# Value products in four 32-row tiles, probabilities without zero blocks, the memory rows turned in two halves, and a new order of the work

## The chip, the cores and the metric

The kernel runs on one core of a Trainium2 chip. The metric is device time in microseconds (us), from start to end of one execution. Engines are called as the profile calls them: PE (matmul) with PEld (its weight loads), DVE (vector), ACT (scalar), POOL (GpSimd) and SP, which issues most DMAs.

## The reference

Sequence 2048, model width 512, 32 heads of 128, memory of 8 rows, segments of 32 rows. The attention is recurrent over 64 segments: each segment attends over its own rows and 8 memory rows, and the first 8 output rows are the memory of the next one.

```python
for s in range(n_seg):                       # 64 segments, one after the other
    xs = x[:, s * seg_len:(s + 1) * seg_len, :]
    h = jnp.concatenate([mem, xs], axis=1)   # 8 + 32 rows
    q, k, v = [jnp.einsum('btd,dhe->bhte', h, W) for W in (Wq, Wk, Wv)]
    scores = jnp.einsum('bhqe,bhke->bhqk', q, k) * scale
    scores = jnp.where(mask[None, None], scores, -1000000000.0)   # memory rows see the memory; all else is causal
    p = _softmax(scores, axis=-1)
    o = jnp.einsum('bhqk,bhke->bhqe', p, v)
    o = jnp.einsum('bhte,hed->btd', o, Wo)
    mem = o[:, :M, :]
    outs.append(o[:, M:, :])
...
h  = x + _A_ref(_layernorm(x), ...)
h2 = h + _B_ref(_layernorm(h), ...)          # layernorm again, w1 (512 x 1792), gelu, w2
```

The mask line of the reference is `(idx[:, None] < M) | (idx[:, None] >= idx[None, :])`: memory rows see every key of their segment, the others see the keys up to their own.

## The kernel before

**Phases.** From 0 to about 44 us the weights arrive. From about 44 to 717 us the 64 segments run, one every 10.3 us. The rest is the second half of the network (w1, gelu, w2) over all rows.

**A segment.** A segment's work on PE is a list of named parts, all in program order on PE:

- `Q0`, `K0`, `Q1`, `K1`, `V0`, `V1`: the projections, by halves of 16 heads. Each is four passes, one for each 128-row chunk of the width; a pass is four matmuls of 512 columns in four 32-column tiles of the array (L872; L605 where the weights of the pass before are kept). `hT` holds the segment's 32 rows turned: 24 rows of x that come early, and 8 memory rows that come from the segment before.
- `SC0`, `SC1` (L1037): the scores of the 8 memory rows, 16 heads each. Their softmax is `sc_softmax`: maximum, two exponentials on ACT with their sums (L1054), reciprocals (L1059), normalized probabilities `PC` (L1062), and a 32x32-blockwise transpose on DVE into `PTC` (L1064).
- `PV0`, `PV1` (`pv_c`, L1075 and L1080): probabilities times values for the memory rows. `VS` holds the values with the keys of four groups of heads on the partitions, 32 each. The products are made in two 64-row tiles of the array; `PC` therefore holds two groups side by side with the other group's block at zero (`even`), and each product has 32 columns (16 wanted and 16 that pair with the zero block), or 128 for the eight rows that come from the next segments' block (`VBD`). The results lie in banks 0 and 1 of the PSUM tile `quad`. One copy brings the memory rows to `OT` (`OTm`), one brings rows of the last part of each segment to `OTB`.
- `SA` (L1105): scores of the 24 x rows, whose softmax ends in `PA` on POOL (L1126), a transpose to `PTA` on DVE (L1128), and four POOL copies (L1132) that lay out `BD`, block-diagonal with zeros. `PVA` (`pv_a`, L1143) multiplies it with the values of the segment before, in 64-row tiles, 48 columns each, into banks 2 and 3; two copies (`OTx0`, `OTx1`) bring it to `OT`. It runs one segment late; the x rows of `OT` are used in `WO` another segment later.
- `WO` (L1171): the output projection, eight units of eight matmuls of 256 columns. Units 0 to 3 need `OTm0`, units 4 to 7 `OTm1`. Its result lies in bank 7. DVE transposes all 256 columns (L1183) and adds the two halves into the memory rows of the next segment's `hT` (L1177, two instructions); this releases the next `Q0`.
- `F0`, `F1`: passes for a whole block of rows (four segments), which no segment waits for at once. They fill PE's time where a chain on the other engines is under way.

**What sets the order.** `ORDERS` has one list for each of four segments in turn (called orders 0 to 3 here), by which PE's parts are cut and laid in a row: `('F1', 2, 3)` is pass 2 of `F1`. The other engines' operations are put in order by a planner (`schedule`): it takes operations by the key of `PLAN`, puts each in the first gap of its engine by modelled durations, and where an operation may run on several engines takes the earliest end, unless `HOME` names one. `op` derives every wait from the tiles and PSUM banks read and written; a bank counts as one thing, and a reader of a bank holds it against later readers too. SC0 and SC1 lie in banks 3 and 2. Banks of the rest: `BANK` (L42), where `K0`, `V0` and `WO` share bank 7.

**Instruction blocks.** PE's instructions are counted (`align`) in blocks of 256; `PHASE` says at which place in a block a segment is to begin, and extra weight loads (L870) pad towards it.

## Time and profile before

| What | Value |
|---|---|
| Time, median of 3 runs | 807.96 us (807.1 to 808.1) |
| Profiled execution: span from first to last instruction | 805.9 us |
| Profiled execution's own time | not listed beside its span; the runs lie 1.2 to 2.2 us above that span |
| PE busy | 775.0 us, 96% of the span |
| DVE busy | 621.0 us, 77% |
| ACT busy | 527.1 us, 65% |
| POOL busy | 349.6 us, 43% |
| Mean granted PE clock | 0.993 |

A busy PE is not a PE at its peak: matmuls overlap in the pipeline, and a matmul that takes 380 ns from start to end occupies its place in the stream for a much shorter time. So pieces of PE's work are measured here from the start of one to the start of the next. A line of a timeline gives the start and the length of a merged piece, engine, source line, operation, the tile written and the tiles read, and how many instructions were merged.

### The profile page before, as it was taken

To read this page: it belongs to the slowest core of one execution; us is meant where nothing else is said; L and a number is where in the kernel's file an instruction comes from. 1 tells how busy PE (TensorE), PEld (TensorE's weight loads), DVE (VectorE), ACT (ScalarE), POOL (GpSimd) and SP (SyncE) were. 2 spreads that over 40 slices of the span, in tenths; PEclk is the share of its full clock that TensorE was granted. 3 is DMA by queue.
4 is the path that set the end of the run, shared out by engine and by line. 5 is a ranking of instruction groups with operands and counts; after the bars stand their busy time and mean duration, and the time that the engine had idled before them with its cause. 6 is when DMAs were issued, how large, how long until landed. Compare 5 with 4: busy or idle time off the path is not lost.

```text
span 805.9 us, 43594 instructions
## 1 busy us (share of the span) xinstructions
PE 775.0 (96%) x19308; PEld 422.5 (52%) x18891; DVE 621.0 (77%) x2008; ACT 527.1 (65%) x1522; POOL 349.6 (43%) x886
## 2 busy tenths in 40 slices
PE   3788999999999999999999999999999999999998
PEld 1345555555555555555555555555555555544443
DVE  3268897989898989898989898989899887824211
ACT  2446777777777777777777777777676766643342
POOL 5023334545454545454545454545463535267200
PEclk9989999999999999999999999999999999999999
DMA  9950010111101010101010202020212131264200
GB/s 340 392 185 16 4 29 11 30 31 29 31 21 39 17 43 17 43 11 50 9 45 10 50 11 50 11 49 3 51 29 62 40 86 29 88 170 130 69 27 26
DMA packets 65449, 48.03 MB, mean 60 GB/s; under 512 B 29028, under 2 KB 61676, under 8 KB 65260
## 3 DMA queue, kind: packets, MB, share of 16 engines
q1 hardware_dynamic: 64928, 44.98, 19.0%
q8 instruction: 150, 2.46, 1.2%
q14 instruction: 39, 0.32, 0.1%
q10 hardware_dynamic: 332, 0.27, 0.1%
HBM read 31.08 MB, written 8.13 MB: 49 GB/s over the span
## 4 chain that ended last, share of the span: by engine, by line
PE 91%; DVE 3%; DMA 2%; SPq 2%; ACT 1%; issue 1%; POOL 0%
PE ps L872 43%; PE ps L1171 16%; PE ps L605 6%; PE quad L1579 6%; PE ps L1572 5%; PE ps L1210 4%; PE quad L1075 3%; DMA WQ<-in_A_Wq_dram 2%; SPq L775 2%; PE ps L1105 2%; PE quad L1037 2%; PE ps L1365 2%; PE quad L1143 1%; PE quad L1080 1%; DVE PC L1062 1%; ACT kq L890 1%
## 5 line engine op out<-in xcount | busy, mean ns | idle before, releaser
L872 PE MATMUL ps<-WQ,hT 128*32 128x512 bf16 x2048 | 157.4, 382 | 3.4 <-DVE hT L1177 3.3
L1171 PE MATMUL ps<-WO,OT 128*32 128x256 bf16 x4224 | 140.8, 275 | 1.0 <-ACT OT L890 1.0
L872 PE MATMUL ps<-WV,hT 128*32 128x512 bf16 x1780 | 138.7, 379 | 0.0
L891 ACT ACTIVATE kq<-ps 128x512 bf16<-128x512 f32 x146 | 87.2, 597 | 63.7 <-PE ps L872 63.4
L1126 POOL TENSOR_TENSOR PA<-SA,rsa 128x256 bf16<-128x256 f32 x64 | 39.9, 624 | 183.0 <-DVE rsa L1119 170.6
L890 ACT CAST kq<-ps 128x512 bf16<-128x512 f32 x160 | 93.4, 584 | 38.2 <-PE ps L872 38.2
L1171 PEld LDWEIGHTS ps<-WO,OT 128*32 128x32 bf16 x4224 | 96.2, 97 | 26.5 <-ACT OT L890 12.3
L1132 POOL COPY BD<-PTA 32x192 bf16<-32x192 bf16 x256 | 95.5, 373 | 16.6 <-DVE PTA L1128 0.8
L1062 DVE SCALAR_TENSOR_TENSOR PC<-EC,rsc,even 128x128 bf16<-128x128 f32 x256 | 94.5, 370 | 6.7
L872 PE MATMUL ps<-WK,hT 128*32 128x512 bf16 x1292 | 92.5, 379 | 0.0
L872 PEld LDWEIGHTS ps<-WQ,hT 128*32 128x32 bf16 x2048 | 57.0, 96 | 57.9 <-issue 18.7
L913 DVE STREAM_TRANSPOSE KALL<-kq 128x256 f32<-128x256 f32 x160 | 70.5, 440 | 20.8 <-ACT kq L890 18.6
L1054 ACT ACTIVATE EC<-quad,nmc 128x64 f32<-128x64 f32 x252 | 77.1, 311 | 5.9 <-DVE nmc L1045 0.2
L605 PE MATMUL ps<-WK,hT 128*32 128x512 bf16 x756 | 74.6, 379 | 0.0
L890 ACT CAST VS<-ps 128x512 bf16<-128x512 f32 x126 | 73.7, 585 | 0.7
L890 ACT CAST OT<-quad 128x128 bf16<-128x128 f32 (+1 forms) x205 | 66.3, 363 | 7.5 <-PE quad L1080 5.7
L913 DVE STREAM_TRANSPOSE QT<-kq 128x256 f32<-128x256 f32 x128 | 57.0, 445 | 15.5 <-ACT kq L891 14.1
L872 PEld LDWEIGHTS ps<-WV,hT 128*32 128x32 bf16 x1780 | 50.5, 96 | 34.2 <-issue 1.0
L1575 ACT ACTIVATE WQ<-ps,b1t 128x512 bf16<-128x512 f32 x42 | 28.9, 688 | 52.0 <-PE ps L1572 52.0
L872 PEld LDWEIGHTS ps<-WK,hT 128*32 128x32 bf16 x1292 | 36.4, 97 | 46.1 <-issue 20.1
L1117 ACT ACTIVATE SA<-SA 128x256 f32<-128x256 f32 x64 | 26.7, 417 | 49.4 <-DVE SA L1116 45.0
L1223 POOL TENSOR_TENSOR opT<-TTB,TTS 32x64 bf16<-32x64 f32 x128 | 40.3, 315 | 31.7 <-DVE opT L1177 22.5
(160 smaller groups left out, 1477.9 us busy)
## 6 DMA issues: line engine op xcount, KB each, us to landing
WV<-in_A_Wv_dram SPq DMA_DIRECT2D x4, 1024.0 KB, 10.3
WK<-in_A_Wk_dram SPq DMA_DIRECT2D x4, 1024.0 KB, 18.0
WQ<-in_A_Wq_dram SPq DMA_DIRECT2D x4, 1024.0 KB, 19.0
WO<-in_A_Wo_dram SPq DMA_DIRECT2D x16, 256.0 KB, 7.6
v_last<-VSB SPq DMA_DIRECT2D x60, 64.0 KB, 3.1
VBD<-v_last SPq DMA_DIRECT2D x60, 64.0 KB, 2.8
h_mid<-xr SPq DMA_DIRECT2D x16, 128.0 KB, 1.8
WQ<-h_mid SPq DMA_DIRECT2D x4, 512.0 KB, 4.4
```

What stands on the lines that cost most here:

```text
L605: return e.add_instruction(mybir.InstMatmult(name="I-%d" % (4000000 + _kept[0]), engine=mybir.EngineType.PE, start_tensor_calc=start, stop ...
L872: ins = e.matmul(o, l, m, start=(k == 0), stop=(k == DC - 1), tile_position=(0, 32 * j), skip_group_check=True)
L890: return {"act": (lambda e: e.copy(out, src), t_act(n, ps_)), "dve": (lambda e: e.tensor_copy(out, src), 0.155 + 1.0e-3 * n * fast)}
L891: return {"act": (lambda e: e.mul(out, src, scale_), t_act(n, ps_)), "dve": (lambda e: e.tensor_scalar(out, src, scale_, None, ALU.mult), ...
L913: S.op("dve", lambda e: e.transpose(out, src), reads=[("kq", i)], writes=[key], dur=t_dve(256) + 0.02)
L1054: return e.activation(EC[:, r, sl, :], o[:, sl, :], ACTF.Exp, bias=nmc[:, r, sl:sl + 1], accum_out=smc[:, r, sl:sl + 1])
L1062: S.op("dve", lambda e, sl=sl, xc=xc: e.scalar_tensor_tensor(PC[:, r, :, :, sl], xc, rsc[:, r, sl:sl + 1], ev, ALU.mult, ALU.mult), reads= ...
L1132: S.narrow(S.op("pool", lambda e, j=j, rows=rows: e.tensor_copy(BD[rows, par, :, j, :, :], PTA[rows, :, 0:NA, :]), reads=["PTA"], writes=[ ...
L1171: ins = e.matmul(ps[bank][32 * j:32 * j + 32, 0:256], lhs(slot(h)), wo_cols(h, b), start=(k == 0), stop=(k == 15), tile_position=(0, 32 * ...
L1223: return e.tensor_tensor(o[32 * q:32 * q + 32, c:c + 2], x, y, ALU.add)
L1572: ins = e.matmul(ps[bank][:, 0:SBT], W1[:, cc, fc * P:(fc + 1) * P], hnT_of(k)[:, cc, :], start=(cc == 0), stop=(cc == DC - 1))
L1579: S.op("pe", lambda e: e.matmul(quad[:, t, :], gT_of(k, fc)[:, t * P:(t + 1) * P], W2[:, fc, :], start=(fc == 0), stop=(fc == FC - 1)), re ...
```

## The change

1. `pv_c` and `pv_a` work in four 32-row tiles, each with a bank of `quad` of its own: 16 products of 16 columns and 4 of 64 for each `PV` (before: 8 of 32 and 2 of 128), 32 of 24 for `PVA` (before: 16 of 48). `PC` and `PTC` are half as wide and have no zero blocks; `BD`, its four POOL copies and `even` are gone, and `PVA` reads `PTA`.
2. `PV0`, `PV1` and `PVA` now write all four banks. `PVA` runs ahead of `PV0`; its two copies run after `PV1`, between `OTm1` and `OTB`.
3. `WO`'s result is turned and added in two halves of two chunks (`TT2`): `hTl`, then `hTm`; each pass waits for its chunk's half alone.
4. In `k_seg` the second half of the keys is copied and turned in two pieces (`KSPLIT`).
5. `ORDERS`, `PLAN`, `HOME`, `PHASE` and `SLIP` are new. `WO` is in one piece behind `PV1`; in orders 0 and 3 three F passes instead of four stand behind `WO`; the prefills of SA are named for DVE in orders 0, 2 and 3.

```diff
-FETCH_AT, PADS, SLIP = 65, 8, 24
-PHASE = (0, 64, 128, 192)
+FETCH_AT, PADS, SLIP = 65, 8, 80
+PHASE = (0, 128, 0, 128)
+TT2, KSPLIT, PCTS, NORM2, OTMS = True, True, False, True, False
...
-ORDERS = ((('Q0', 0, 1), ('K0', 0, 1), ('Q0', 1, 2), ('K0', 1, 2), ('Q0', 2, 3), ('Q1', 0, 1), ('Q0', 3, 4), ('K0', 2, 4), ('Q1', 1, 4), ('K1', 0, 4), ('SC0', 0, 99), ('V0', 0, 1), ('V1', 0, 1), ('V0', 1, 4), ('F1', 0, 1), ('SC1', 0, 99), ('V1', 1, 2), ('F1', 1, 2), ('V1', 2, 4), ('F0', 0, 1), ('PV0', 0, 99), ('PVA', 0, 99), ('F1', 2, 3), ('WO', 0, 2), ('PV1', 0, 99), ('WO', 2, 8), ('F1', 3, 4), ('SA', 0, 99), ('F0', 1, 4)),
...
+ORDERS = ((('Q0', 0, 2), ('K0', 0, 3), ('Q0', 2, 4), ('K0', 3, 4), ('Q1', 0, 4), ('K1', 0, 4), ('SC0', 0, 99), ('V1', 0, 1), ('V0', 0, 4), ('F1', 0, 1), ('SC1', 0, 99), ('F1', 1, 2), ('V1', 1, 4), ('F1', 2, 3), ('F0', 0, 1), ('PVA', 0, 99), ('PV0', 0, 99), ('F1', 3, 4), ('PV1', 0, 99), ('WO', 0, 8), ('F0', 1, 4), ('SA', 0, 99)),
+          (('Q0', 0, 1), ('K0', 0, 2), ('Q0', 1, 4), ('K0', 2, 4), ('Q1', 0, 4), ('K1', 0, 4), ('SC0', 0, 99), ('V1', 0, 1), ('V0', 0, 4), ('F1', 0, 1), ('SC1', 0, 99), ('F1', 1, 3), ('V1', 1, 4), ('PVA', 0, 99), ('PV0', 0, 99), ('F1', 3, 4), ('PV1', 0, 99), ('WO', 0, 8), ('SA', 0, 99), ('F0', 0, 4)),
+          (('Q0', 0, 1), ('K0', 0, 2), ('Q0', 1, 4), ('Q1', 0, 1), ('K0', 2, 4), ('Q1', 1, 4), ('K1', 0, 4), ('SC0', 0, 99), ('V1', 0, 1), ('V0', 0, 4), ('F1', 0, 1), ('SC1', 0, 99), ('V1', 1, 3), ('F1', 1, 3), ('V1', 3, 4), ('PVA', 0, 99), ('PV0', 0, 99), ('F1', 3, 4), ('PV1', 0, 99), ('WO', 0, 8), ('SA', 0, 99), ('F0', 0, 4)),
+          (('Q0', 0, 1), ('K0', 0, 2), ('Q0', 1, 4), ('K0', 2, 4), ('Q1', 0, 4), ('K1', 0, 4), ('SC0', 0, 99), ('F0', 0, 1), ('V0', 0, 4), ('V1', 0, 1), ('SC1', 0, 99), ('V1', 1, 4), ('F0', 1, 4), ('PVA', 0, 99), ('PV0', 0, 99), ('F1', 0, 1), ('PV1', 0, 99), ('WO', 0, 8), ('F1', 1, 2), ('SA', 0, 99), ('F1', 2, 4)))
...
-PLAN = {"kq2": (1.72,) * 4,
...
+PLAN = {"EC0": (-0.197, 2.191, -0.625, -6.415),
...
-HOME = {('SC0', 0): 'act', 'ZCm0': 'pool', 'kq1': 'act', 'SP1': 'act', 'VS1': 'act', 'OTm0': 'act', 'SAp': 'dve', 'PA': 'pool', 'VSB1': 'act'}
+HOME = {'SP1': 'act', 'SAp': 'dve', ('SA', 2): 'dve', 'ZCm1': 'pool', 'OTx0': 'act', 'PA': 'pool', ('SC1', 0): 'act', 'ZCm0': 'pool', ('SA', 0): 'dve', ('SC0', 2): 'act', ('SC1', 3): 'dve', 'kq2': 'act', 'kq0': 'act', ('SA', 3): 'dve', 'VSB1': 'dve', 'OTm1': 'act', 'VSB0': 'act', 'VS0': 'act', 'OTm0': 'act', ('SC0', 0): 'dve'}
...
-        PC = sb("PC", [P, 2, 2, 64, 2])
-        PTC = sb("PTC", [P, 2, 2, 64, 2])
+        PC = sb("PC", [P, 2, 64, 2])
+        PTC = sb("PTC", [P, 2, 64, 2])
-        BD = sb("BD", [P, 2, 4, 4, NA, 2])
...
+        HT = ("hTl", "hTl", "hTm", "hTm") if TT2 else ("hTm",) * 4
+        HK = ("hTl", "hTm") if TT2 else ("hTm",)
...
+            if r == 1 and KSPLIT and s > 0:
+                for h, (a, b) in enumerate((("kql", "KAl"), ("kq", "KA"))):
+                    c = slice(4 * h, 4 * h + 4)
+                    S.either(copy2(kq[:, r, c], ps[bank][:, 256 * h:256 * h + 256].rearrange("p (a b e) -> p a e b", a=4, b=2), 256), reads=[("ps", bank)], writes=[(a, r)])
+                    src = kq[:, r, c].rearrange("p a e b -> p a (e b)").bitcast(F32)
+                    S.op("dve", lambda e, h=h, src=src: e.transpose(words(KALL[:, a0 + 4 * h:a0 + 4 * h + 4]), src), reads=[(a, r)], writes=[(b, par, r)], dur=0.31)
+                return
...
-            for sl, names in enumerate((("Ea", "sa", "ra", "PCa"), ("EC", "smc", "rsc", "PC"))):
-                ek, sk, rk, pk = [(n, r) for n in names]
-                S.op("dve", lambda e, sl=sl: e.reciprocal(rsc[:, r, sl:sl + 1], smc[:, r, sl:sl + 1]), reads=[sk], writes=[rk], dur=0.16)
-                x = EC[:, r, sl, :]
-                xc = bass.AP(x.tensor, x.offset, [list(x.ap[0]), [0, 2], [1, 64]])
-                S.op("dve", lambda e, sl=sl, xc=xc: e.scalar_tensor_tensor(PC[:, r, :, :, sl], xc, rsc[:, r, sl:sl + 1], ev, ALU.mult, ALU.mult),
-                     reads=[ek, rk, "even"], writes=[pk], dur=0.305)
-            S.op("dve", lambda e: e.transpose(PTC[:, r].rearrange("p k t a -> p (k t a)").bitcast(F32), PC[:, r].rearrange("p k t a -> p (k t a)").bitcast(F32)),
-                 reads=[("PCa", r), ("PC", r)], writes=[("PTC", r)], dur=0.31)
+            if NORM2:
+                for sl, names in enumerate((("Ea", "sa", "ra", "PCa"), ("EC", "smc", "rsc", "PC"))):
+                    ek, sk, rk, pk = [(n, r) for n in names]
+                    S.op("dve", lambda e, sl=sl: e.reciprocal(rsc[:, r, sl:sl + 1], smc[:, r, sl:sl + 1]), reads=[sk], writes=[rk], dur=0.16)
+                    f = lambda e, sl=sl: e.tensor_scalar(PC[:, r, :, sl], EC[:, r, sl, :], rsc[:, r, sl:sl + 1], None, ALU.mult)
...
+            S.op("dve", lambda e: e.transpose(PTC[:, r].rearrange("p t a -> p (t a)").bitcast(F32), PC[:, r].rearrange("p t a -> p (t a)").bitcast(F32)),
+                 reads=[("PC", r)] + [("PCa", r)] * NORM2, writes=[("PTC", r)], dur=0.25)
...
-                    for t in range(2):
-                        rows = slice(64 * t, 64 * t + 64)
+                    for j in range(4):
+                        rows = slice(32 * j, 32 * j + 32)
                         c0 = 16 * (i % 2)
-                        o = quad[:, t, 128 * r:128 * r + 128].rearrange("p (b i q) -> p i b q", b=2, i=4)[:, i]
-                        e.matmul(o, VS[rows, s % 3, r, i * E:(i + 1) * E], PTC[rows, r, :, c0:c0 + 16, i // 2],
-                                 start=(r == 0 and i == 0), stop=False, tile_position=(64 * t, 0), skip_group_check=True)
-                for t in range(2):
-                    rows = slice(64 * t, 64 * t + 64)
-                    o = quad[:, t, 128 * r:128 * r + 128].rearrange("p (b a q) -> p b a q", b=2, a=2)
-                    ins = e.matmul(o, VBD[rows, bk % 2, sg, r, :], PTC[rows, r, :, 32:64, :].rearrange("p b q a -> p b a q"),
-                                   start=False, stop=True, tile_position=(64 * t, 0), skip_group_check=True)
+                        e.matmul(quad[:, j, 64 * r + 16 * i:64 * r + 16 * i + 16], VS[rows, s % 3, r, i * E:(i + 1) * E], PTC[rows, r, c0:c0 + 16, i // 2],
+                                 start=(s == 0 and r == 0 and i == 0), stop=False, tile_position=(32 * j, 0), skip_group_check=True)
+                for j in range(4):
+                    rows = slice(32 * j, 32 * j + 32)
+                    o = quad[:, j, 64 * r:64 * r + 64].rearrange("p (a x) -> p a x", a=2)
+                    ins = e.matmul(o, VBD[rows, bk % 2, sg, r, :], PTC[rows, r, 32:64, :].rearrange("p x a -> p a x"), start=False, stop=True, tile_position=(32 * j, 0), skip_group_check=True)
                 return ins
-            S.op("pe", f, reads=[("VS", s % 3, r), ("PTC", r)] + [("VBD", bk % 2, j) for j in range(4)], writes=CQ, dur=0.205, mode=MH, ni=20)
-            src = bass.AP(quad[:].tensor, quad[:].offset + 128 * r, [list(quad[:].ap[0]), [512, 2], [16, 8], [1, MEM]])
-            ot = OT[:, par, :, NA:SEG].rearrange("p (t r k) q -> p r t k q", t=2, r=2)[:, r]
-            S.either(copy2(ot, src, 128), reads=CQ, writes=[("OTm", par, r)])
+            S.op("pe", f, reads=[("VS", s % 3, r), ("PTC", r)] + [("VBD", bk % 2, j) for j in range(4)], writes=QK, dur=0.205, mode=MR, ni=40)
+            for k, (b0, nb) in enumerate(((0, 2), (2, 2)) if OTMS else ((0, 4),)):
+                src = quad[:, b0:b0 + nb, 64 * r:64 * r + 64].rearrange("p j (i q) -> p j i q", i=4)[:, :, :, 0:MEM]
+                ot = OT[:, par, :, NA:SEG].rearrange("p (j r i) q -> p r j i q", j=4, r=2)[:, r, b0:b0 + nb]
+                S.either(copy2(ot, src, 32 * nb), reads=QK[b0:b0 + nb], writes=[("OTm", par, r) if k == 0 else ("OTn", par, r)])
         def pv_c_b(s):
             bk, sg = s // 4, s % 4
-            src = bass.AP(quad[:].tensor, quad[:].offset + MEM, [list(quad[:].ap[0]), [512, 2], [16, 16], [1, 8]])
-            ot = OTB[:, bk % 2, :, 8 * sg:8 * sg + 8].rearrange("p (t k) q -> p t k q", t=2)
-            S.either(copy2(ot, src, 256), reads=CQ, writes=[("OTB", bk % 2, sg)])
+            src = quad[:, :, 0:128].rearrange("p j (x q) -> p j x q", q=16)[:, :, :, MEM:16]
+            ot = OTB[:, bk % 2, :, 8 * sg:8 * sg + 8].rearrange("p (j x) q -> p j x q", j=4)
+            S.either(copy2(ot, src, 256), reads=QK, writes=[("OTB", bk % 2, sg)])
...
-            for j in range(4):
-                rows = slice(32 * j, 32 * j + 32)
-                S.narrow(S.op("pool", lambda e, j=j, rows=rows: e.tensor_copy(BD[rows, par, :, j, :, :], PTA[rows, :, 0:NA, :]), reads=["PTA"], writes=[("BD", par, j)], dur=0.42))
...
-                    for t in range(2):
-                        rows = slice(64 * t, 64 * t + 64)
-                        c0 = 192 * (k // 4) + 24 * (k % 4)
-                        o = quad[:, 2 + t, c0:c0 + 120].rearrange("p (b q) -> p b q", q=24)[:, 0:5:4]
-                        ins = e.matmul(o, VS[rows, par, k // 4, (k % 4) * E:(k % 4 + 1) * E], BD[rows, s % 2, k // 2, 2 * t:2 * t + 2, :, k % 2],
-                                       start=(k == 0), stop=True, tile_position=(64 * t, 0), skip_group_check=True)
+                    for j in range(4):
+                        rows = slice(32 * j, 32 * j + 32)
+                        ins = e.matmul(quad[:, j, 128 + 24 * k:152 + 24 * k], VS[rows, par, k // 4, (k % 4) * E:(k % 4 + 1) * E], PTA[rows, k // 2, 0:NA, k % 2],
+                                       start=(k == 0), stop=True, tile_position=(32 * j, 0), skip_group_check=True)
                 return ins
-            S.op("pe", f, reads=[("VS", par, 0), ("VS", par, 1)] + [("BD", s % 2, j) for j in range(4)], writes=AQ, dur=0.29, mode=MH, ni=32)
+            S.op("pe", f, reads=[("VS", par, 0), ("VS", par, 1), "PTA"], writes=QK, dur=0.29, mode=MR, ni=64)
         def pv_a_ev(s):
             for t in range(2):
-                src = quad[:, 2 + t, 0:384].rearrange("p (k q) -> p k q", q=24)
-                S.either(copy2(OT[:, s % 2, 16 * t:16 * t + 16, 0:NA], src, 384), reads=[("ps", 2 + t)], writes=[("OTx", s % 2, t)])
+                src = quad[:, 2 * t:2 * t + 2, 128:320].rearrange("p j (k q) -> p j k q", q=24)
+                ot = OT[:, s % 2, 16 * t:16 * t + 16, 0:NA].rearrange("p (j k) q -> p j k q", j=2)
+                S.either(copy2(ot, src, 384), reads=[("ps", 2 * t), ("ps", 2 * t + 1)], writes=[("OTx", s % 2, t)])
...
-            if mem:
-                sl = (s + 1) % RING
-                S.op("dve", lambda e: [halves_add(tt, q2, hT[64 * q2:64 * q2 + 64, sl, :, NA:SEG], slice(NA, SEG))(e) for q2 in range(2)][1],
-                     reads=[("TT", par)], writes=[("hTm", sl)], dur=0.4)
+            for h, k_ in enumerate(("TTl", "TT") if TT2 else ("TT",)):
+                w, c = (2, slice(2 * h, 2 * h + 2)) if TT2 else (4, slice(0, 4))
+                S.op("dve", lambda e, h=h, w=w, c=c: e.transpose(tt[:, c].rearrange("p c q t -> p (c q t)"), ps[bank][:, 128 * h:128 * h + 64 * w]), reads=[("ps", bank)], writes=[(k_, par)],
+                     dur=0.3 if TT2 else t_dve(256) + 0.02)
+                if mem:
+                    sl = (s + 1) % RING
+                    S.op("dve", lambda e, c=c: [halves_add(tt, q2, hT[64 * q2:64 * q2 + 64, sl, c, NA:SEG], slice(NA, SEG), c)(e) for q2 in range(2)][1],
+                         reads=[(k_, par)], writes=[(HK[h], sl)], dur=0.36 if TT2 else 0.4)
             if xrows:
...
                     pv_c(s, r)
                     if r == 1:
+                        if s > 0:
+                            t_, S.tag = S.tag, (s, "PVAE")
+                            pv_a_ev(s - 1)
+                            S.tag = t_
                         pv_c_b(s)
...
```

183 lines of the change are left out of this document (92 added, 91 removed), and 3 rows, old and new, of the table ORDERS.

## The prediction

> **What bounds the kernel now.** I read the page first, then the busy times of a stretch of ten segments, then PE's timeline of one segment, then the groups of the operations that the change touches.
>
> ```profile
> span 805.9 us, 43594 instructions
> PE 775.0 (96%) x19308; PEld 422.5 (52%) x18891; DVE 621.0 (77%) x2008; ACT 527.1 (65%) x1522; POOL 349.6 (43%) x886
> ...
> PE 91%; DVE 3%; DMA 2%; SPq 2%; ACT 1%; issue 1%; POOL 0%
> ...
> 407.00:510.00 103.00, 103.00 (x2928) 58.23 (x2795) 92.76 (x310) 75.10 (x228) 49.77 (x128) 1.00 0.13 31
> ```
>
> The chain that ended last runs 91% over PE. In the stretch (columns: busy PE, PEld, DVE, ACT, POOL, then the clock) PE is never idle, at full clock; DVE is at 90%, ACT 73%, POOL 48%. So a gain must take time out of PE's stream, and busy time alone doesn't show where it waits. The starts in one segment do:
>
> ```profile
> 401.59 0.41 PE L872 MATMUL ps<-WQ,hT 128*32 128x512 bf16 x4
> ...
> 406.47 0.30 PE L1037 MATMUL quad<-KALL,ZC 128*32 128x64 bf16 x16
> ...
> 407.45 0.40 PE L1210 MATMUL ps<-WO,OTB 128*32 128x512 bf16 x4
> 407.79 0.27 PE L1075 MATMUL quad<-PTC,VS 64*128 64x32 bf16 x8
> 407.91 0.22 PE L1080 MATMUL quad<-PTC,VBD 64*128 64x128 bf16 x2
> 407.96 0.36 PE L1143 MATMUL quad<-BD,VS 64*128 64x48 bf16 x16
> 408.25 0.40 PE L1210 MATMUL ps<-WO,OTB 128*32 128x512 bf16 x4
> 408.55 0.62 PE L1171 MATMUL ps<-WO,OT 128*32 128x256 bf16 x16
> 409.11 0.27 PE L1075 MATMUL quad<-PTC,VS 64*128 64x32 bf16 x8
> 409.22 0.22 PE L1080 MATMUL quad<-PTC,VBD 64*128 64x128 bf16 x2
> 409.37 1.50 PE L1171 MATMUL ps<-WO,OT 128*32 128x256 bf16 x48
> ...
> 410.90 0.40 PE L1105 MATMUL ps<-KALL,QT 128*32 128x32 bf16 x32
> 411.13 0.84 PE L1210 MATMUL ps<-WO,OTB 128*32 128x512 bf16 x12
> 411.86 0.41 PE L872 MATMUL ps<-WQ,hT 128*32 128x512 bf16 x4
> ```
>
> From Q0 to Q0 (401.59 to 411.86) is 10.27 us. A pass takes about 0.215: pieces of three passes and of one differ by 0.44, the half of it is 0.22, and I round down since starts within a pass spread. With that, three waits stand in the stream. Before PV0: the pass at 407.45 is streamed at 407.665, going over to the row-tiled products takes 0.10 to 0.12 (next paragraph), PV0 starts at 407.79: 0.02 over. Before WO: 408.25 + 0.215 = 408.465 against 408.55: 0.085. Before Q0: 411.13 + 3 x 0.215 = 411.775 against 411.86: 0.085. Together 0.19 us per segment; this is all that better overlap can win, 12 us over 62 segments.
>
> Change of tiling: WO's four rounds from 408.55 (48 products in 1.50 less their 0.275 tail: 26 ns each, 0.104 a round of four) end at 408.97 to 408.99, PV1 starts at 409.11: 0.12 in. Out: PVA's 16 products end at 408.16, the pass starts at 408.25: 0.09. The change keeps two entries and two exits, so they cancel.
>
> **The change part by part.** The rows for prices:
>
> ```profile
> L1075 PE MATMUL quad<-PTC,VS 64*128 64x32 bf16 x1024 | 34.0, 176 | 3.3 <-DVE rsc L1059 2.3 <-ACT OT L890 0.6 <-DVE PTC L1064 0.2
> L1143 PE MATMUL quad<-BD,VS 64*128 64x48 bf16 x1024 | 23.1, 180 | 0.0
> L1105 PE MATMUL ps<-KALL,QT 128*32 128x32 bf16 x2048 | 26.9, 178 | 0.0
> L1037 PE MATMUL quad<-KALL,ZC 128*32 128x64 bf16 x2016 | 38.1, 193 | 0.2 <-POOL ZC L927 0.2
> L1062 DVE SCALAR_TENSOR_TENSOR PC<-EC,rsc,even 128x128 bf16<-128x128 f32 x256 | 94.5, 370 | 6.7
> L1064 DVE STREAM_TRANSPOSE PTC<-PC 128x128 f32<-128x128 f32 x128 | 39.9, 312 | 4.4
> L1183 DVE STREAM_TRANSPOSE TT<-ps 128x256 f32<-128x256 f32 x66 | 29.2, 443 | 20.6 <-PE ps L1171 20.4
> L1177 DVE TENSOR_TENSOR hT<-TT 64x32 bf16<-64x32 f32 x126 | 24.7, 196 | 3.0
> L1177 DVE TENSOR_TENSOR opT<-TT 64x96 bf16<-64x96 f32 x128 | 33.8, 264 | 3.0
> L1132 POOL COPY BD<-PTA 32x192 bf16<-32x192 bf16 x256 | 95.5, 373 | 16.6 <-DVE PTA L1128 0.8
> L1012 ACT COPY ps<-maskAF 128x256 f32<-128x256 f32 x62 | 25.3, 408 | 0.1
> L890 ACT CAST OTB<-quad 128x256 bf16<-128x256 f32 x63 | 23.5, 373 | 2.0
> ...
> 407.46 0.31 ACT L1054 ACTIVATE EC<-quad,nmc 128x64 f32<-128x64 f32 x1
> 407.75 0.58 ACT L890 CAST VS<-ps 128x512 bf16<-128x512 f32 x1
> 409.48 0.27 ACT L890 CAST OT<-quad 128x128 bf16<-128x128 f32 x1
> ```
>
> *Value products.* A PV takes 407.79 to 407.96, 0.17. Within it the eight products of 32 columns go at (0.27 - 0.176)/7 = 13 ns, two tiles at a time: 27 ns a round. PVA's, of 48 columns, go at (0.36 - 0.18)/15 = 12: 24 a round. So a round costs about 25 whether 32 or 48 columns wide, and the zero columns were nearly free. [...]
>
> The number of rounds stays too: 4 + 1 for a PV, 8 for PVA, with four products in a round. No row has four row tiles. The nearest are four column tiles: SA's 32 products go at (0.40 - 0.178)/31 = 7.2 ns, 29 a round. PV: five rounds of 27 = 0.135 (0.125 to 0.145), the last being 64 columns instead of 128: -0.03, twice -0.06. PVA: between 8 x 24 = 0.19 and 8 x 29 = 0.23; I take 0.21, +0.02. Were the four weight loads of a round made one after the other, at the 12 ns between two products now, PVA would take 0.38 and a PV 0.24: +0.33 in all. That is the far bound. Slots: -0.04.
>
> *Waits that go.* Before PV0: PVA now stands ahead of it, and PTC0 comes earlier: DVE's two `PC` have half the elements (370 each; 64-column DVE rows bound it by 196 to 264, I take 0.2) and the transpose is half (0.312 for 128 columns and 0.443 for 256 make some 0.25 for 64). -0.02. Before WO: `OTm0` is now waited for by PV1. -0.085.
>
> *The wait that comes.* PV1 writes the banks that `OTm0` reads, and one F pass is its whole cover. From PV0's last product: stream 0.03, exit 0.09, pass 0.215, entry 0.12: PV1 could start after 0.455. The copy: the product takes 0.19 from start to end (L1037, 64 columns too), ACT starts 0.04 later (409.22 + 0.22 to 409.48), takes 0.27, and PE hears of it some 0.05 later: 0.55. With all of today's delay, 407.91 to 408.55, it is 0.64. The stall is 0.095 to 0.185; I take 0.11, near the row that no other copy delayed. WO behind it waits for nothing: `OTm1` is due four units (16 rounds of 0.104, the half of them, 0.8) later.
>
> *The memory in halves.* Before: 0.443 + 2 x 0.196 = 0.83 from WO's end to `hT`. `hTl`: a transpose of 128 (0.31) and two additions of 16 columns (0.18 each by the 196 and 264 rows): 0.67, so 0.16 earlier. In orders 1 and 2 the cover stays and the 0.085 go. In orders 0 and 3 one pass (0.215) went ahead of PVA, so the wait grows by 0.055. K0 also writes bank 7, which the second transpose must have read: `hTl` + 0.31, against one or two passes of cover; about 0.1 in the one order where a short tail meets a short head. Mean (-0.085 x 2 + 0.055 x 2 + 0.1)/4 = +0.01: nothing.
>
> *What costs PE nothing.* POOL loses 4 x 0.373 = 1.5 us per segment, but PVA never waited for `BD` (idle 0.0 above). DVE: -4 x 0.17 - 2 x 0.06 for the softmax; +0.18 for the two transposes, +0.33 for the additions, +0.15 for the split keys, +0.41 x 3/4 for SA's prefill: about +0.17, so 92% instead of 90%. It stays hidden as long as the critical pieces come first in DVE's queue. ACT: 2 x 0.373 - 0.58 = +0.16 for the keys, -0.31 for the prefill. PE gets 72 more instructions per segment (40 for a PV instead of 20, 64 for PVA instead of 32), and so some more blocks to fetch; the segment shown, longer than two blocks of 256, has no gap beyond the three waits.
>
> **Sum.** -0.04 - 0.02 - 0.085 + 0.11 + 0.01 = -0.025 per segment; with the bounds of slots (-0.08 to 0.00) and stall, -0.08 to +0.10. The head and the last phase keep their work. What this sum can't see is how the new order uses the memory path, which I now count from SC1: before, its `PTC1` comes late enough that WO had to be cut in two around PV1; softmax (up to -0.40: both `PC` and the transpose) and `hTl` (-0.16) give that path 0.5 us, and PE-side waits of a few hundredths elsewhere in orders 0 to 3 can close. I take -0.02 more, an estimate of a tenth of the old waits: -0.045 x 62 = -2.8 us on 805.9, that is 803.1 for the span; the median lies 2.1 above the span before, so **805**.
>
> **Rivals.**
>
> *ACT is late for the four-bank lock* (slower). Place: the last exponential of SC1, which reads bank 2. Today it ends at 407.77, 1.30 after SC1's start (406.47). PVA, which overwrites bank 2, comes in orders 1 and 2 at 0.12 + 5 x 0.215 + 0.12 = 1.32: no margin. The copies of K1, 0.16 longer in two pieces, stand ahead of the exponentials on ACT, and behind them `VS1` (0.58) holds ACT until the moment PV0's results are ready. It decides from the first hundredth that the exponentials are late, and what they are late adds to PVA or PV1. At 0.16: -0.045 + 0.16 = +0.115, 812. For it: no slack in two of four orders. Against: orders 0 and 3 have a pass more, and DVE takes the prefill off ACT.
>
> *Everything cancels.* PVA at 0.23, PV0 behind it as slow as SA, the stall 0.13 or more: 0 to +0.02, 808.
>
> *Weight loads of four row tiles don't overlap* (slower): +0.33 - 0.045, 823 to 826. Against: two row tiles overlap today.
>
> *The relaxed path is used in full*: of the 0.19 of old waits nearly all go and little comes, -0.13: 798 to 800. For it: the 0.5 us. Against: `OTm0` has one pass of cover in all four orders.
>
> **How the numbers follow.** Forecast 0.40 (own range 802 to 808), ACT and the lock 0.23, cancelling 0.20, relaxed path 0.12, serial loads 0.05. A measurement of this kernel tells about 0.2% (1.6 us) from no change. Faster: 0.12, and 0.36 of the forecast's 0.40: 0.48. Same: 0.18 of cancelling and 0.03 of the forecast: 0.21. Slower: 0.23 + 0.05 + 0.03 of rests: 0.31. The range 797 to 815 takes in the lock and the relaxed path and leaves out the serial loads and the tails.
>
> **What would show it.** Starts of PVA's 32 products 6 to 7.5 ns apart, in row tiles; 12 would be serial loads. PV0's last product to PV1 0.55 us, with ACT's copy as releaser. No wait at WO's first unit. Transposes of `PTC` and of WO's halves at 0.25 to 0.31; Q0 right behind the F passes in segments that follow orders 1 and 2. PVA right behind its pass: if it starts over 0.15 late, released by ACT, the lock is the cause. Wrong would be a segment under 10.1 us or over 10.4, or a PE that waits for DVE at K0 or SC1.

## The result, and the profile after

The changed kernel takes **854.1 us** (median of 4 runs, 850.8 to 860.9); the kernel before, run beside it, takes 808.0. The ratio is 1.058 (95% interval [1.053, 1.062]): 46 us slower, where 3 us faster was forecast. One execution of one kernel below, at a granted clock of 0.56, took 1292.7 us and is left out of its ratio.

The page of the changed kernel, its profiled execution (850.8 us):

```profile
span 849.1 us, 47781 instructions
...
PE 789.7 (93%) x21621; PEld 427.6 (50%) x20776; DVE 627.8 (74%) x2273; ACT 543.8 (64%) x1575; POOL 247.5 (29%) x621
...
q8 instruction: 166, 2.72, 1.3%
...
PE 68%; DVE 11%; ACT 11%; issue 4%; DMA 2%; SPq 2%; POOL 2%
```

The same stretch of 103 us as before (columns: busy PE, PEld, DVE, ACT, POOL, then the clock):

```profile
407.00:510.00 103.00, 98.05 (x3048) 54.02 (x2852) 87.55 (x326) 72.66 (x219) 31.67 (x82) 1.00 0.11 26
```

At the same full clock PE now stands idle for 5 of 103 us, and DVE has fallen from 90% to 85%. The chain that ended last runs 68% over PE instead of 91%; DVE and ACT have 11% each, and 4% is "issue", time in which the engine waited for nothing that the profile shows. The q8 row counts instruction packets of 16 KB: 166, where the kernel before has 150. PE's products and loads, 42397 here and 38199 before, make 255 a packet in both, so I take the packets for PE's blocks of 256.

From the start of SA in the second segment, at 60.40 us, to that in the last, at 743.05, a segment takes 11.01 us ((743.05 - 60.40)/62); before it was 10.32. Segments are very uneven, 9.6 to 14.7. PE's timeline of one:

```profile
435.53 0.83 PE L1222 MATMUL ps<-WO,OTB 128*32 128x512 bf16 x12
436.29 0.37 PE L1151 MATMUL quad<-PTA,VS 32*128 32x24 bf16 x32
436.51 0.24 PE L1088 MATMUL quad<-PTC,VS 32*128 32x16 bf16 x9
437.26 0.21 PE L1088 MATMUL quad<-PTC,VS 32*128 32x16 bf16 x7 [0.52 <-issue]
437.31 0.21 PE L1093 MATMUL quad<-PTC,VBD 32*128 32x64 bf16 x4
437.45 0.40 PE L1222 MATMUL ps<-WO,OTB 128*32 128x512 bf16 x4
437.89 0.26 PE L1088 MATMUL quad<-PTC,VS 32*128 32x16 bf16 x16
438.00 0.20 PE L1093 MATMUL quad<-PTC,VBD 32*128 32x64 bf16 x4
438.13 1.93 PE L1180 MATMUL ps<-WO,OT 128*32 128x256 bf16 x64
439.88 0.39 PE L1222 MATMUL ps<-WO,OTB 128*32 128x512 bf16 x4
440.10 0.31 PE L1118 MATMUL ps<-KALL,QT 128*32 128x32 bf16 x24
441.38 0.23 PE L1118 MATMUL ps<-KALL,QT 128*32 128x32 bf16 x8 [0.96 <-issue]
```

PV0 stops after 9 of its 16 products and goes on 0.75 us after it began; SA stops after 24 of 32, and its last eight come 1.28 us after its start. Nothing that PE waits for stands between two products of one loop, and no engine releases them. The waits of PE over 60 to 700 us (engine, line, what it waited for: us in total, times, longest):

```profile
PE ps L1118 <- issue: 5.5, 11, 1.0
PE ps L875 <- issue: 4.0, 7, 1.2
PE ps L1222 <- issue: 2.6, 3, 1.2
PE quad L1088 <- issue: 1.6, 3, 0.6
PE quad L1093 <- issue: 0.4, 1, 0.4
PE ps L1180 <- issue: 0.3, 1, 0.3
```

These are 14.4 us in 26 waits. The same view of the kernel before lists five rows, 5.4 us in all, each with an engine that releases it, and none of this kind. The two locks on the quad's four banks show at the weight loads that begin `PVA` and PV1:

```profile
436.29 0.27 PEld L1151 LDWEIGHTS quad<-PTA,VS 32*128 32x128 bf16 x32 [0.42 <-ACT EC L1062]
...
437.88 0.17 PEld L1088 LDWEIGHTS quad<-PTC,VS 32*128 32x128 bf16 x16 [0.33 <-ACT OT L893]
```

A PEld wait counts from the last weight load, so the pass that still streams (some 0.2) is in it. To compare kernels I therefore use PE alone: wherever a product starts over 0.215 us after the one before it, between 60 and 700 us, I sum what exceeds 0.2 (one pass), by what released it. I call this the **gap sum**. A change of tiling, 0.106, is in it: where nothing holds them, `PVA` starts 0.312 us after the last product of the pass ahead, and SA, which changes nothing, 0.206. Before: 23.9 us, of which 10.5 stand ahead of PV0 (62 times, for its softmax), 5.3 ahead of WO (for `OTm0`), 6.0 ahead of Q0 (for the memory). After: 57.8, of which 15.7 stand ahead of PV1 (58 times, for `OTm0`), 12.4 ahead of `PVA` (58 times, for the last exponential), and 15.0 have no releaser. (Two of the expectations below count a little differently: 16.4 and 14.3 for `OTm0` and the exponential. In the kernel before, the change of tiling ahead of PV1 falls just under the limit and isn't counted.)

### The profile page after: what moved, and what is told of

Read it like the earlier page. It is cut to its first block, busy times and chain, and to the rows that moved or that the text cites. A ratio compares the mean times of both kernels' runs of the same rounds, so it can differ in the third digit from the quotient of the medians.

```text
span 849.1 us, 47781 instructions
## 1 busy us (share of the span) xinstructions
PE 789.7 (93%) x21621; PEld 427.6 (50%) x20776; DVE 627.8 (74%) x2273; ACT 543.8 (64%) x1575; POOL 247.5 (29%) x621
## 4 chain that ended last, share of the span: by engine, by line
PE 68%; DVE 11%; ACT 11%; issue 4%; DMA 2%; SPq 2%; POOL 2%
PE ps L875 24%; PE ps L1180 15%; PE quad L1591 6%; PE ps L613 5%; PE ps L1584 4%; ACT EC L1062 4%; PE quad L1088 3%; PE ps L1222 3%; PE quad L1151 2%; DMA WQ<-in_A_Wq_dram 2%; ACT kq L893 2%; SPq L775 2%; ACT OT L893 2%; PE ps L1118 2%; PE ps L1377 2%
## 5 line engine op out<-in xcount | busy, mean ns | idle before, releaser
L875 PE MATMUL ps<-WV,hT 128*32 128x512 bf16 x1844 | 134.2, 379 | 0.0
L1180 PE MATMUL ps<-WO,OT 128*32 128x256 bf16 x4224 | 132.7, 276 | 0.6 <-issue 0.3
L875 PE MATMUL ps<-WQ,hT 128*32 128x512 bf16 x1544 | 121.3, 380 | 3.4 <-DVE hT L1186 3.2
L893 ACT CAST kq<-ps 128x256 bf16<-128x256 f32 (+1 forms) x223 | 103.3, 463 | 28.5 <-PE ps L875 24.9
L875 PE MATMUL ps<-WK,hT 128*32 128x512 bf16 x1544 | 117.8, 379 | 0.2 <-DVE hT L1186 0.2
L1180 PEld LDWEIGHTS ps<-WO,OT 128*32 128x32 bf16 x4224 | 107.5, 97 | 12.2 <-issue 3.7
L937 POOL COPY ZC<-QT 128x128 bf16<-128x128 bf16 x126 | 36.7, 291 | 241.8 <-DVE QT L916 241.1
L893 ACT CAST OT<-quad 128x128 bf16<-128x128 f32 (+1 forms) x238 | 82.1, 365 | 37.3 <-PE quad L1093 32.9
L875 PEld LDWEIGHTS ps<-WQ,hT 128*32 128x32 bf16 x1544 | 42.1, 96 | 66.6 <-issue 22.2
L875 PEld LDWEIGHTS ps<-WK,hT 128*32 128x32 bf16 x1544 | 44.2, 96 | 62.0 <-issue 28.2
L1194 DVE STREAM_TRANSPOSE TT<-ps 128x128 f32<-128x128 f32 x132 | 41.7, 316 | 41.6 <-PE ps L1180 39.3
L875 PEld LDWEIGHTS ps<-WV,hT 128*32 128x32 bf16 x1844 | 51.4, 97 | 33.2 <-issue 1.6
L1069 DVE TENSOR_SCALAR PC<-EC,rsc 128x64 bf16<-128x64 f32 x256 | 60.8, 262 | 4.0
L613 PE MATMUL ps<-WQ,hT 128*32 128x512 bf16 x504 | 52.1, 379 | 0.0
```

The costliest lines, as they stand in the source:

```text
L613: return e.add_instruction(mybir.InstMatmult(name="I-%d" % (4000000 + _kept[0]), engine=mybir.EngineType.PE, start_tensor_calc=start, stop ...
L875: ins = e.matmul(o, l, m, start=(k == 0), stop=(k == DC - 1), tile_position=(0, 32 * j), skip_group_check=True)
L893: return {"act": (lambda e: e.copy(out, src), t_act(n, ps_)), "dve": (lambda e: e.tensor_copy(out, src), 0.155 + 1.0e-3 * n * fast)}
L1069: f = lambda e, sl=sl: e.tensor_scalar(PC[:, r, :, sl], EC[:, r, sl, :], rsc[:, r, sl:sl + 1], None, ALU.mult)
L1180: ins = e.matmul(ps[bank][32 * j:32 * j + 32, 0:256], lhs(slot(h)), wo_cols(h, b), start=(k == 0), stop=(k == 15), tile_position=(0, 32 * ...
L1194: S.op("dve", lambda e, h=h, w=w, c=c: e.transpose(tt[:, c].rearrange("p c q t -> p (c q t)"), ps[bank][:, 128 * h:128 * h + 64 * w]), rea ...
```

## The experiments

Two causes were at hand: PE's instruction blocks come late (called late blocks below), and the four-bank lock. The first four kernels set each against the kernel before.

**64 weight loads more per segment, in the passes.**

```diff
-PHASE = (0, 64, 128, 192)
+PHASE = (0, 128, 0, 128)
```

> The kernel before with about 64 more weight loads per segment on PE, spread over the projection passes, which leave PE's queue room. Theory (blocks of 256 PE instructions come no sooner than about 3.5 us after the block before was entered; the dense stretches are as before): within 0 to 5 us of before, 808 to 813. Rival (each PE instruction costs its issue, about 3.5 ns): 64 x 62 x 3.5 ns = +14 us, 822. Rival (what counts is the number of instructions per segment, 640 as in the changed kernel): +20 us or more.

Measured: 815.9 us, ratio 1.010 [1.008, 1.012]: 7.5 us, more than the 0 to 5 of the theory, half of what the price by issue asked (1.9 ns a load, where it took 3.5), and far from the 20 of a price by number alone. No wait without a releaser is over 0.15 us.

**The same number of loads more, in WO.** Each weight load of WO is made twice.

```diff
-PHASE = (0, 64, 128, 192)
+PHASE = (0, 128, 0, 128)
...
+                                e.ldweights(lhs(slot(h)), tile_position=(0, 32 * j))
```

> The kernel before with the same number of additional weight loads (64 per segment), each weight of WO's 64 products loaded twice, so that they stand in the densest stretch. Theory of late instruction blocks: stalls of 0.3 to 0.5 us per segment that no semaphore releases, each ending some 2.4 us after the start of an instruction fetch: 828 to 838. Rival (the changed kernel lost its time to the bank locks and the new order alone; additional instructions are hidden): 808 to 812. Rival (a second load lengthens each WO product): pieces of WO longer throughout, with no stalls.

Measured: 842.2 us, 1.043 [1.041, 1.045], above the 828 to 838 expected. The two kernels fetch 166 and 167 packets, the changed one 166, and they compute the same products; what differs is where the loads stand. In the passes, where each stands beside 0.05 us of streaming, they cost 7.5 us, in WO, where the products are 26 ns apart, 34. The second load itself costs next to nothing: WO's two pieces take 0.354 and 1.228 us from first to last product in the median segment, in the kernel before 0.348 and 1.222. PE's waits with WO's loads doubled, in a kernel whose tiles, banks and orders are those of before:

```profile
PE ps L1172 <- issue: 6.1, 16, 0.5
PE ps L872 <- issue: 4.5, 11, 0.8
PE ps L605 <- issue: 0.5, 1, 0.5
```

So the waits without a releaser come of instructions that stand too thick, and not of their number alone. These rows sum to 11.1 us of the 34. The view leaves out breaks under 0.15 us, and where the rest lies is not shown.

**The lock alone.** The 64-row tiles of before, but `PVA` ahead of PV0, its copies behind PV1, and every value product holding all four banks.

```diff
-..., reads=[("VS", s % 3, r), ("PTC", r)] + ..., writes=CQ, dur=0.205, mode=MH, ni=20)
+..., reads=[("VS", s % 3, r), ("PTC", r)] + ..., writes=QK, dur=0.205, mode=MH, ni=20)
...
-... for j in range(4)], writes=AQ, dur=0.29, mode=MH, ni=32)
+... for j in range(4)], writes=QK, dur=0.29, mode=MH, ni=32)
```

> The kernel before with 64-row tiles and 576 instructions, but with PVA ahead of PV0, PVA's copies behind PV1, and each of PV0, PV1 and PVA holding all four banks. Theory of the lock: PVA waits for SC1's last exponential and WO for OTm0 behind one pass: 0.2 to 0.4 us per segment, 820 to 833, with no stall that nothing releases. Rival (the locks are harmless, the loss is all instruction blocks): 808 to 811.

Measured: 831.0 us, 1.028 [1.027, 1.030]. No product waits without a releaser; the weight loads of `PVA` and WO wait for ACT:

```profile
PEld quad L1143 <- ACT EC L1054: 38.6, 60, 1.0
...
PEld ps L1171 <- ACT OT L890: 20.2, 60, 0.5
```

In the kernel before, the first row is absent and the second has 12.0 us, 61 times. The lock costs 22.6 us in the old order, as its theory said (820 to 833).

**The tiles alone.** The changed value products (four row tiles, no zero blocks) in the orders and plan of before with `PVA` ahead; no cuts in halves.

> The changed value products (32-row tiles, narrow probabilities, no BD) in the order and plan of the kernel before with PVA ahead of PV0; no halves of WO's output, no split keys. Theory (locks and late blocks add up): b_lock plus 0.35 to 0.5 us per segment, 845 to 860. Rival (only the new order and plan are bad): 810 to 822. Rival (four row tiles load their weights one after the other): the products of PVA start 12 ns apart, and 0.33 us per segment come without stalls at block starts.

Measured: 859.7 us, 1.063 [1.061, 1.065]: 28.7 us above the lock alone. From that kernel it differs by the tiles, by cheaper DVE and POOL work, and by 90 PE instructions a segment (the trace has 665 products and loads a segment against 575): 72 of the products, and 18 more weight loads that pad towards the block boundaries. At the price of the first experiment, 7.5 us for 64, the 18 would cost some 2 us, an estimate. Waits without a releaser are back:

```profile
PE ps L1217 <- issue: 4.6, 11, 0.8
PE ps L870 <- issue: 3.8, 10, 0.7
PE ps L1175 <- issue: 3.5, 4, 1.0
```

With three shorter rows these are 13.2 us in 28 waits; where the rest of the 28.7 lies is not shown. The two causes add up, and the work saved with the zero blocks doesn't make up for it.

The next runs start from the changed kernel.

**Block boundaries moved.**

```diff
-FETCH_AT, PADS, SLIP = 65, 8, 80
-PHASE = (0, 128, 0, 128)
+FETCH_AT, PADS, SLIP = 65, 8, 24
+PHASE = (64, 192, 64, 192)
```

> The changed kernel with only the place of the 256-instruction block boundaries moved by about 64 instructions against its operations (other PHASE, fewer pads). Late-blocks theory: gaps of PE that nothing in the trace releases stay in number (30 to 45) and sum (10 to 22 us), but stand at other operations than in the changed kernel; 845 to 863 us. Rival (these gaps belong to the operations, such as the four row tiles or SA, whatever the block): they stay at the same lines and the time stays at 852 to 856. Rival (locks alone): no difference at all.

Measured: ratio 1.056 [1.053, 1.058], as the changed kernel. Contrary to the expectation this kernel has more pads, 14 a segment against 5. Its waits are read from one more execution:

> The changed kernel with its block boundaries moved by about 64 instructions, a profile at full clock. Late-blocks theory: 30 to 45 gaps that nothing releases, 10 to 22 us, at other lines than in the changed kernel. Rival: at the same lines.

Measured: 852.6 us, and PE's waits:

```profile
PE ps L1118 <- issue: 10.6, 22, 0.9
PE ps L1180 <- issue: 2.4, 8, 0.4
PE ps L1222 <- issue: 1.8, 4, 0.6
PE quad L1088 <- issue: 1.8, 2, 1.0
PE quad L1093 <- issue: 1.2, 2, 0.6
PE ps L613 <- issue: 0.2, 1, 0.2
```

39 waits, 18.0 us. The passes of L875 have lost theirs (4.0), WO and SA have more. By lines this is a mixed answer: the waits move, but SA stays the chief place, which I had not expected. It stands at the end of the thickest stretch, and I take this for the reason.

The distances between the waits decide it. In the segment shown above, the stretch from the break in PV0 to the break in SA holds 7 + 4 + 4 + 16 + 4 + 64 + 4 + 24 = 127 products with as many loads: 254 instructions, one block of 256 but for two that the timeline doesn't list. The same count between each of the 26 waits of the changed kernel and the next, divided by the packets that start in between, gives 253 to 255.3 in all 25 cases, also where the two stand at different operations (PV0 and SA, SA and WO, WO and SA). With the boundaries moved it is 251 to 257.5 in all 38. So the waits stand at the block boundaries, and not at the operations as such.

**Fewer products.** Half of SA's products are left out, and `PVA` has one of 48 columns for two of 24. The padding weight loads, five a segment in the changed kernel, are left out as well.

```diff
-PHASE = (0, 128, 0, 128)
+PHASE = ()
...
-                for k in range(8):
+                for k in range(0, 8, 2):
...
-                        ins = e.matmul(quad[:, j, 128 + 24 * k:152 + 24 * k], ..., PTA[rows, k // 2, 0:NA, k % 2],
+                        ins = e.matmul(quad[:, j, 128 + 24 * k:176 + 24 * k]..., ..., PTA[rows, k // 2, 0:NA, :]...,
```

> The changed kernel with 64 PE instructions fewer per segment: SA leaves out every second head's product, and PVA makes one product of 48 columns in place of two of 24 (half of its heads get another head's values). That is 576 instructions a segment, as in the kernel before; locks, orders and the other engines stay. By count of rounds it saves 4 rounds of 29 ns and 4 of 25 ns, 0.21 us a segment, 13 us: 841. Late-blocks theory: the unreleased gaps (about 18 us in all) go to under 5 us as well: 822 to 832. Rival (the gaps come from the form of the products, not from the number of instructions): 838 to 846, gaps still over 12 us.

Measured: 833.7 us, 1.032 [1.029, 1.035], just above the theory's 822 to 832. Among PE's waits one row of the kind is left; the largest is another:

```profile
PE quad L1088 <- DVE PTC L1077: 10.8, 42, 1.4
...
PE ps L875 <- issue: 1.5, 3, 0.7
```

So with fewer instructions the waits go, though four row tiles and the lock stay, and WO with doubled loads has them with the old tiles. The time, however, fell by 20 us only: 13 are the rounds left out, by the estimate above, and where 13 us of waits went only 7 more were won, so at least 5 came back elsewhere. The gap sum ahead of Q0, for the memory, rose from 3.4 to 11.2, ahead of K0, for WO's second transpose, from 2.1 to 5.5, and ahead of PV1 from 15.7 to 20.9, now mostly for `PTC1`. SA is a good quarter of the cover that the memory path has in two orders (SA and three passes), and the late blocks had been part of that cover too.

**SC1 off the quad.** Scores of the second half in bank 4 (6 in one order), the plan and `HOME` made anew, and in order 0 one F pass exchanged.

```diff
-            bank_of = OPEN_BANK if s == 0 else BANK
+            bank_of = OPEN_BANK if s == 0 else dict(BANK, SC1=4 if sg < 3 else 6)
```

> The changed kernel with SC1's scores in bank 4 (bank 6 in one order of four) in place of the quad's bank 2, the plan of the other engines made anew, one order's F0 pass moved from ahead of PVA to behind PV0. Lock theory: the wait of PVA for ACT's last exponential (14.3 us in the changed kernel) falls to under 4 us, the wait of PV1 for OTm0 (16.4 us) stays or grows a little, the late blocks stay: 838 to 850. Rival (the lock only passes the wait on, as PTC1 or the next release is late anyway): 850 to 860, with the wait at PV1 or WO grown by about the 14 us.

Measured: 853.9 us, 1.058 [1.055, 1.061]: the rival. `PVA` lost its wait (gap sum 12.4 to 6.6, of which 58 x 0.106 = 6.1 are the change of tiling), PV1 gained (15.7 to 26.3). The weight loads show the same:

```profile
PEld quad L1088 <- ACT OT L893: 31.0, 57, 1.1
```

**Two passes over the copy.** In addition one F pass goes from ahead of `PVA` to between PV0 and PV1; for one order:

```diff
-('F1', 1, 3), ('V1', 1, 4), ('PVA', 0, 99), ('PV0', 0, 99), ('F1', 3, 4), ('PV1', 0, 99)
+('F1', 1, 2), ('V1', 1, 4), ('PVA', 0, 99), ('PV0', 0, 99), ('F1', 2, 4), ('PV1', 0, 99)
```

> The kernel with SC1 off the quad, and one F pass moved from ahead of PVA to between PV0 and PV1, so that two passes (0.43 us) instead of one stand over the copy of OTm0. Lock theory: the copy takes some 0.55 us from PV0's end, two passes with entry and exit take 0.67, so the wait of PV1 (24.8 us in all with one pass) falls to about 10, of which 6.5 are the change of tiling, nothing of like size comes at PVA, and the late blocks stay: 838 to 846. Rival (the wait is passed on again, to PVA or PV0 for PTC0 and the last PC of DVE): PVA or PV0 gains what PV1 loses, 850 to 856.

Measured: 856.3 us, 1.058 [1.055, 1.061]: the rival again. PV1's gap sum fell from 26.3 to 12.0, near what the lock theory said. But the weight loads of the `PV`s (L1085) now wait 10.3 us for `PTC`, where it was 2.1, and those of `PVA` (L1148) wait for `PC`:

```profile
PEld quad L1085 <- ACT OT L890: 20.2, 40, 1.0
PEld quad L1148 <- DVE PC L1066: 17.0, 40, 0.4
PEld quad L1085 <- DVE PTC L1074: 10.3, 21, 1.0
```

A pass moved along the chain from the scores over softmax and `PTC` to the copies moved the wait: PV0 now starts 0.23 us after `PVA`'s last product in the mean, against 0.10 with SC1 off the quad alone, which is 7 us of the 14 that PV1 lost. And PE's waits without a releaser rose from 9.6 us to 15.1.

The last three took the halves.

**The halves in the kernel before.** WO's output in two halves and K1's keys in two pieces, tiles and orders of before.

> The kernel before (64-row tiles, its own orders and plan) with only the two cuts in halves: WO's output turned and summed in two halves, K1's keys evicted and turned in two pieces. My forecast's terms for them: +0.01 us a segment, 808 to 809. Rival (DVE's and ACT's added time, some +0.7 and +0.16 us a segment, is not hidden in the old order): Q1 waits for SA's softmax to have read its bank, 812 to 826. Rival (the earlier memory half closes the wait before Q0): 802 to 805.

Measured: 845.4 us, 1.047 [1.045, 1.048], far over every expectation: 38 us. What the first rival named, Q1 and SA's softmax, is what the next kernel shows; its price was too low.

**The memory's halves alone, in the kernel before.** As above, with the keys whole.

> The kernel before with WO's output turned and summed in two halves, K1's keys left whole. It tells which of the two cuts made the 37 us of both together. By DVE's instructions the memory's halves add 0.48 us a segment (two transposes for one, four additions for two), the keys' halves 0.15 on DVE and 0.16 on ACT. If the cost goes by DVE's time: 830 to 840. If it is the keys (Q1 waiting for what stands behind them): 808 to 816.

Measured: 840.6 us, 1.040 [1.038, 1.042], just above what the price by DVE's time gave. PE never waits without a releaser for more than 0.2 us; its weight loads wait for the reads of SA's softmax on DVE:

```profile
PEld ps L877 <- DVE SA L1121: 42.0, 55, 0.8
```

The old orders start Q1 after three passes of Q0 and two of K0, in the bank that SA's scores lie in; two transposes and four additions now stand ahead of their reads in DVE's queue. This alone is 32 us; the keys add 6.

**The halves undone in the changed kernel.**

```diff
-FETCH_AT, PADS, SLIP = 65, 8, 80
+FETCH_AT, PADS, SLIP = 65, 8, 140
...
-TT2, KSPLIT, PCTS, NORM2, OTMS = True, True, False, True, False
+TT2, KSPLIT, PCTS, NORM2, OTMS = False, False, False, True, False
```

> The changed kernel with its two cuts in halves undone (WO's output turned and summed as one, K1's keys as one); tiles, orders and the plan of the other engines stay. If the halves cost by themselves what they cost in the kernel before (37 us there), this comes out near 817 to 835. My forecast's term (nothing, +0.01 us a segment): 852 to 856. Theory: the new orders are built on the earlier half, two of them have no pass between SA and Q0 but SA itself; without it Q0 waits 0.16 us or more for the memory in most segments, while DVE's freed time wins little: 858 to 872.

Measured: 861.2 us, 1.065 [1.063, 1.066], inside what the theory said: the new orders put Q1 behind all of Q0 and K0 (but for one pass of Q1 in order 2), and there the halves are worth 7 us. Not all of it need be theirs: PE's waits for the memory in `hT` rose from 2.5 to 6.5 us, but those without a releaser rose as well, from 14.4 to 18.3.

## Why the prediction was wrong, by its steps

**The step that failed.** "PE gets 72 more instructions per segment ... and so some more blocks to fetch; the segment shown, longer than two blocks of 256, has no gap beyond the three waits" priced the instructions at nothing. What it said was true of the segment shown, and no bound for the changed one. Before, 576 instructions in 10.3 us use up a block every 4.6 us. The thickest stretch decides: the same 64 loads cost 34 us in WO and 7.5 in the passes. In the segment shown of before, PV0 to SA's end is 280 instructions (20 + 32 + 8 + 32 + 20 + 96 + 8 + 64) in 3.3 us (407.79 to 411.13), 12 ns each. In the segment shown above the same parts are 352 (64 + 40 + 8 + 40 + 128 + 8 + 64) in 5.14 us (436.29 to 441.43), of which some 1.9 are the two breaks and PV1's wait: without them 3.2 us, 9 ns each. In the old order the runs put the tiles with their instructions at 28.7 us (tiles alone against the lock alone), of which the 18 pads may be some 2. In the changed kernel the waits at block boundaries are 14.4 us. The step should have asked how thick the instructions come, and it had the numbers to.

That PE waits for its blocks is seen in the packets too. Around one wait of the changed kernel, on PE's timeline and by the DMA queues of the window from 416.0 to 419.0:

```profile
417.44 0.40 PE L875 MATMUL ps<-WQ,hB 128*32 128x512 bf16 x2
418.49 1.04 PE L875 MATMUL ps<-WQ,hB 128*32 128x512 bf16 x14 [0.65 <-issue]
```

```profile
q8 instruction: 1, 0.02, 2.0%
```

The one packet starts at 416.05, 2.44 us ahead of the wait's end; the next starts at 419.54, 1.05 behind it. All 26 waits without a releaser of the changed kernel end 2.3 to 2.9 us after the start of a packet, and the next packet starts 1.0 to 1.7 us later; from packet to packet these are 3.36 us at least, 3.62 in the middle.

**The lock.** The rival "ACT is late for the four-bank lock" named a real wait, though not its whole price. `PVA` in the segment shown starts on time (435.53 + 3 x 0.215 + 0.12 = 436.295, against 436.29), with six passes behind SC1 in this order; over all segments its gap sum less the change of tiling is 12.4/58 - 0.106 = 0.11 us. By orders, the median segment has it on time in orders 0 and 3 and 0.13 and 0.15 late in orders 1 and 2 (0.440 and 0.464 after the pass's last product, less 0.312), just the two that the rival named, at 0.16. (The rival's price was a slip: +0.115 over 62 segments is 7 us on 808, so 815 and not 812.) PV1's stall was forecast at 0.11 (0.095 to 0.185): 437.45 + 0.215 + 0.12 = 437.785 against 437.89 is 0.105 in the segment shown, the mean is 15.7/58 - 0.106 = 0.16. The mechanism was right, the size low by 0.05. By these two the lock would make 0.27 us a segment, 17 us, less 0.15 of the old waits before PV0 (10.5/62 - 0.106 = 0.06) and WO (5.3/62 = 0.09), which went as forecast: some 8 us net, where the terms of the forecast, +0.11 - 0.02 - 0.085, made nothing. In the old order the lock made 22.6.

**The slots** came out as forecast. The groups of the two lines:

```profile
L1088 PE MATMUL quad<-PTC,VS 32*128 32x16 bf16 x2048 | 36.3, 170 | 11.6 <-DVE PTC L1077 3.1 <-ACT OT L893 2.5 <-issue 1.6
L1151 PE MATMUL quad<-PTA,VS 32*128 32x24 bf16 x2048 | 23.5, 170 | 5.7 <-ACT EC L1062 3.3 <-DVE PTC L1077 0.5
```

One product takes 0.17 us from start to end. `PVA`'s 32 products go at (0.37 - 0.17)/31 = 6.5 ns, 26 a round, 0.21 in all; PV1's 16 at (0.26 - 0.17)/15 = 6, 24 a round. Four row tiles load their weights side by side: one load takes 91 ns, and `PVA`'s 32 loads take 0.27 us in the segment shown, one every 6 ns. So the rival of serial loads falls, and a round of 16 or 24 columns costs what one of 32 or 48 did: the narrowing bought nothing, at twice the instructions.

**The other engines.** The prices, from the groups of the changed kernel:

```profile
L1069 DVE TENSOR_SCALAR PC<-EC,rsc 128x64 bf16<-128x64 f32 x256 | 60.8, 262 | 4.0
L1186 DVE TENSOR_TENSOR hT<-TT 64x16 bf16<-64x16 f32 x252 | 44.1, 175 | 5.9
L1194 DVE STREAM_TRANSPOSE TT<-ps 128x128 f32<-128x128 f32 x132 | 41.7, 316 | 41.6 <-PE ps L1180 39.3
L1077 DVE STREAM_TRANSPOSE PTC<-PC 128x64 f32<-128x64 f32 x128 | 30.7, 241 | 3.3
```

`PC` was taken at 0.2 and takes 0.262; the others are within 0.01 of the forecast. DVE's 92% was not reached, since the segments grew. The halves' +0.01 was wrong in both directions: worth some 7 us in the new order, a cost of 38 in the old. What decided was the condition that the forecast named, that the critical pieces come first in DVE's queue, and which bank waits behind them.

**The sum.** In the old order, lock 22.6 and tiles with their instructions 28.7 make 51.3 of loss; the halves, orders and plan of the change win some 5 back, and 46 remain. How the 46 split between lock and blocks within the new order was not settled: the waits cover one another, as the fewer products and the two runs on the lock show.

## What to carry to other kernels

Where PE's work is made of short products, count instructions per microsecond over the thickest stretch, weight loads included, before splitting a product into more and narrower ones: here a finer tile that kept the number of rounds saved nothing (24 to 26 ns a round, before 24 to 27) and doubled the instructions. When products that had banks of their own come to share all of them, every reader of the old results can become a wait (22.6 us here, in the old order), and moving cover along one chain may only move the wait. A cut in halves that shortened one path here lengthened the queue for the others (38 us in the old order): look for what stands behind it, and try it in the order it will run in.

## What the runs showed that was not expected

- PE's instruction blocks have a period in these traces. Where PE waits for one in the changed kernel, 3.4 to 4.5 us pass from packet to packet, 3.6 in the middle, though a packet itself takes only 0.9 to 1.5: about 14 ns for an instruction. The least distance of two packets is 3.28 us there, and 3.37 in the kernel before. WO's products and loads, 128 in 1.75 us (438.13 to 439.88), come at just that rate; a round of value products, eight in 25 ns, is four times as fast. Why the kernel before, at 12 ns over its thickest stretch, has no such wait is not shown.
- The same 64 added weight loads per segment cost 7.5 us in the passes and 34 in WO.
- A wait can be of use: with most of the late blocks gone, part of their time came back as waits for the memory path (the gap sum ahead of Q0 rose from 3.4 to 11.2 us).
